# The last chunk as a whole of 512 queries, and W2's load behind the transposes of chunk 1

## The chip, the cores and the metric

The kernel runs on one core of a Trainium2 chip. The core has five engines with an instruction stream each: PE (TensorE, matrix products), DVE (VectorE), ACT (ScalarE), POOL (GpSimd) and SP (SyncE, which here only issues DMAs). PE's weight loads (PEld) run beside its matmuls. Each engine works through its own stream in order; between engines, an instruction waits for semaphores. The metric is the device time of one execution in microseconds, as a median over runs.

## What is computed

Four layers over x of 2048 rows and 512 columns, in bf16 inputs: attention, feed-forward, and the same two again with the same weights. Each adds to x the result of its layer on a normalised x.

```
x = x + A(layernorm(x));  x = x + B(layernorm(x))      # and both once more
A: q, k, v = x @ wqkv (512 x 1536), 32 heads of 16
   scores = q k^T / 4, query i sees keys i-255 .. i    # a sliding window of 256
   softmax over the keys, times v, then @ wo (512 x 512)
B: relu(x @ w1) @ w2                                    # 512 -> 1792 -> 512
```

## The kernel before

**Steps.** The 2048 rows are four chunks of 512 (NCH = 4, L80). Two layers of four chunks make eight steps, k = 0 to 7 (NSTEP, L83). A step is: normalise and transpose the chunk (plan_qkv, L462: xn, then a DMA transpose into xnT), project it to K, Q and V, attend (plan_attention, L532), and then plan_rest (L589): transpose O, multiply by wo, add to x, normalise and transpose again (xn2T), W1 with a ReLU into hT, W2, and add to x, or in the second layer write to the output as ob.

**Attention.** Heads are taken eight at a time (t = 0 to 3). A Unit (L37) is one t for all eight 64-query blocks of a chunk (nq = 8, table FULL, L21) or for half a chunk (nq = 4, table HALF, L28). The tables cut the visible key blocks of a unit into groups: five in FULL, three in HALF. A group is a set of small score matmuls into Sps (all four banks of it), one exponential on ACT from Sps into Pb, and masks on DVE or POOL that zero what the window excludes. Since Sps exists once, the scores of a group wait for the exponential of the group before. When the groups of a unit are masked, P·V matmuls go into a PSUM bank acc, and DVE divides by the sum of the row into O. The two Pb buffers alternate from unit to unit, so a unit's exponentials wait for the P·V matmuls of the unit two before.

The tuple HALVED (L421) names the steps that are attended as two halves of 256 queries: units for all t of the first half, then all t of the second. The same tuple cuts the feed-forward of these steps (L634): W1 is done for columns n0 to n1 of xn2T, 256 or 512 wide, 14 f-blocks of four matmuls each; then W2 for the blocks of 128 rows in that half, 14 matmuls each. In the last step the transposes of O and of xn are done on PE and not by DMA (final, L601).

**Order of work.** Nothing is put in order by hand. Every piece of work is an op (L222) with the engines that could do it, a duration for each as the author estimates it, what it depends on, and a key. A list scheduler in the kernel (from L692) plays the program through with these durations when the program is built, and each engine takes the ready op with the smallest key (on PE) or the smallest time plus key (elsewhere). What it decides is the order in which instructions are written to each engine, and on the chip this order is kept. Scores come before everything on PE (key -1e5), then P·V, then the output projection; projections and feed-forward have keys counted in score groups (first_slot, base), so that they fill PE between groups. The feed-forward of a step has keys from base[k + 1] + 9 to base[k + 1] + 28, that is, during the attention of the next step; the halved one has d0 from its own step's units (L636). K, Q and V of a step have keys 16 groups ahead of the units that need them. Where the scheduler finds PE idle, it writes a dummy matmul (warm, L792).

Limits that the scheduler knows are pools of buffers: four PSUM banks for everything but scores, three xn buffers (L227), three stg, three OT. hT and xn2T exist once, so W1 of a step waits for W2 of the step before. A load is modelled as landed at a fixed time (L231 to L240); such a time only shapes the order, while the chip waits for the DMA itself.

**Loads.** All of x, wqkv, wo, W1 and W2 are loaded at the start by DMAs issued on SP (L131 to L142), in this order: x of chunk 0 in two parts, the three parts of wqkv, x of chunks 1 to 3, wo, W1, W2. The DMA transposes of xn, O and the second xn are issued on SP too. Every matmul and every other instruction goes through one wrapper at L106, so all rows of the profile have that line, and are told apart by their tiles: W1 and W2 are both "w" there, as the program's names are shown without their numbers, W1's matmuls being `ps_d<-xn2T,w` and W2's `ps_d<-w,hT`.

Of the kernel before, what the change touches and what calls it, by code (L numbers as in the profile page):

```python
# [15 lines left out]
P = 128  # L16
# [46 lines left out]
def kernel(  # L63
# [19 lines left out]
    NSTEP = 2 * NCH  # L83
# [31 lines left out]
    pe, dve, act, pool, sp = (InOrder(x) for x in (nc.tensor, nc.vector, nc.scalar, nc.gpsimd, nc.sync))  # L115
# [23 lines left out]
    w1 = const.tile([P, KC, DFF], BF16, name="w1")  # L139
    sp.dma_start(w1[:], B_w1.rearrange("(kc p) n -> p kc n", p=P))  # L140
    w2 = const.tile([P, NF, D], BF16, name="w2")
    sp.dma_start(w2[:], B_w2.rearrange("(f p) n -> p f n", p=P))  # L142


    ident = const.tile([P, P], BF16, name="ident")
# [76 lines left out]
    def op(key, opts, deps=(), take=None, uses=(), keep=0):  # L222
        uses = list(uses) + ([take] if take is not None and take not in uses else [])
        return Op(key, opts, deps, take, uses, keep)
# [6 lines left out]
    def landed(t):  # L231
        o = Op(0, {}, [], None, [], 0)
        fixed.append((o, t))
        return o
# [2 lines left out]
    d_x = [landed(3.95), landed(4.5)]  # L237
    d_w = {1: landed(7.4), 0: landed(9.0), 2: landed(10.6)}
    d_xc = {c: landed(11.4 + 1.7 * c) for c in range(1, NCH)}
    d_wo, d_w1, d_w2 = landed(18.0), landed(24.0), landed(30.0)  # L240


    def copy(e, o, i, relu=False):
# [174 lines left out]
        dve.tensor_tensor(out=x_sb[:, b, :], in0=ps, in1=x_raw(b, b + 1)[:, 0, :] if raw else x_sb[:, b, :], op=ALU.add)  # L418


    HALVED = (0, NSTEP - 1)  # L421
    units, base = [], []
    for k in range(NSTEP):
        base.append(sum(len(u.groups) for u in units))
        for q0, nq in ((0, 4), (4, 4)) if k in HALVED else ((0, 8),):
            units += [Unit(k, k % NCH, t, q0, nq) for t in range(4)]
# [27 lines left out]
    applied, turned = {}, {}  # L454
# [134 lines left out]
    def plan_rest(k):  # L589
# [43 lines left out]
        w1_mm[k], w2_mm[k] = [], []  # L633
        for j0, j1 in ((0, 2), (2, 4)) if k in HALVED else ((0, 4),):  # L634
            if k in HALVED:
                d0 = first_slot[units_of[k][3 + 2 * j0]] + 8  # L636
# [36 lines left out]
    for k in range(NSTEP):  # L673
        plan_attention(k)
        if k == 0:
            plan_qkv(1)
        plan_rest(k)
        if 0 < k < NSTEP - 1:
            plan_qkv(k + 1)
# [274 lines left out]
```

## Time and profile before

| What | us |
|---|---|
| median of 8 runs | 488.06 (485.29 to 488.9) |
| the profiled execution: time | 487.32 |
| the profiled execution: span, first to last instruction | 485.6 |
| PE busy, share of the span | 464.2, 96% |
| DVE / ACT / POOL busy | 367.9 / 337.6 / 316.5 |
| mean granted PE clock | 0.994 |

A row of a timeline or a group reads: start, duration, engine, line, operation, what it writes <- what it reads, shapes, how many; in brackets how long the engine had stood idle before it, and what ended the wait. "<-DMA xnT<-xn" is a DMA transpose that landed. Matmuls overlap, so the spacing between them is shorter than the duration of one. A row of a table of stretches gives, for each engine, its busy time in that stretch with the number of instructions, then the granted PE clock and the share of the DMA engines. SPq rows are DMA issues, and their time is that of issuing, not of the transfer.

### The profile page before, as it was taken

The numbers are of one execution on the slowest core, as the hardware profiler recorded it, in microseconds if no ns is written. First come the engines' busy times: TensorE is split into PE (matmuls) and PEld (weight loads), VectorE is DVE, ScalarE is ACT, GpSimd is POOL, SyncE is SP. The second block draws the span as 40 slices with busy tenths as digits, with TensorE's granted clock in tenths as the row PEclk, the third lists the DMA queues.
The fourth block names the chain that finished last, engine by engine and source line by source line (L and its number), as shares of the span: only waits on it lengthen the run. The fifth ranks groups of instructions, "written<-read, shape, count | busy, mean of one in ns | idle before, by whom it ended". The sixth has DMA issues, their size and how long they took to land.

```text
span 485.6 us, 14677 instructions
## 1 busy us (share of the span) xinstructions
PE 464.2 (96%) x6055; PEld 249.6 (51%) x6055; DVE 367.9 (76%) x965; ACT 337.6 (70%) x281; POOL 316.5 (65%) x716
## 2 busy tenths in 40 slices
PE   7879899998999999999999999999999999999995
PEld 3544555654445545554554554555555455554662
DVE  6969989858898789878989977898758878463111
ACT  3858877878678767876778877777875676755340
POOL 7768878768886788767878767677656557631000
PEclk9989999999999999999999999999999999999999
DMA  8951141004310052002221114020143002100100
GB/s 267 371 58 23 25 66 24 3 1 55 59 22 3 13 78 45 3 1 45 56 36 25 21 31 50 12 46 1 24 88 57 13 1 45 36 12 13 34 23 28
DMA packets 54652, 22.00 MB, mean 45 GB/s; under 512 B 46129, under 2 KB 54065, under 8 KB 54577
## 3 DMA queue, kind: packets, MB, share of 16 engines
q1 hardware_dynamic: 54576, 20.98, 20.4%
q8 instruction: 49, 0.80, 0.7%
q14 instruction: 27, 0.21, 0.2%
HBM read 7.86 MB, written 2.10 MB: 21 GB/s over the span
## 4 chain that ended last, share of the span: by engine, by line
PE 73%; DVE 10%; DMA 7%; POOL 5%; ACT 2%; issue 2%; ACTq 0%; POOLq 0%; DVEq 0%
PE ps_d L106 52%; PE acc L106 12%; PE Sps L106 8%; DMA OT<-O 4%; POOL Pb L106 2%; DMA xnT<-xn 2%; ACT Pb L106 2%; DVE st L106 2%; DVE KBD L106 1%; POOL xn L106 1%; DVE V2f L106 1%; DVE xn L106 1%; DVE Pb L106 1%; DMA xn2T<-xn 1%; DVE Vst L106 1%
## 5 line engine op out<-in xcount | busy, mean ns | idle before, releaser
L106 ACT ACTIVATE Pb<-Sps 128x2048 bf16<-128x2048 f32 (+4 forms) x164 | 283.9, 1731 | 96.2 <-PE Sps L106 72.8
L106 POOL TENSOR_SCALAR_AFFINE_SELECT Pb<-Pb 64x256 bf16<-64x256 bf16 x526 | 226.4, 430 | 96.2 <-ACT Pb L106 73.5
L106 PE MATMUL ps_d<-xn2T,w 128*128 128x512 bf16 (+1 forms) x560 | 110.5, 337 | 1.3 <-DVE hT L106 0.9
L106 PE MATMUL ps_d<-w,hT 128*128 128x512 bf16 x448 | 110.0, 380 | 0.0
L106 PEld LDWEIGHTS <-Pb 128*128 128x128 bf16 x2880 | 83.4, 96 | 24.3 <-issue 7.8
L106 PE MATMUL acc<-V2f,Pb 128*128 128x34 bf16 x2880 | 89.9, 178 | 2.0 <-POOL Pb L106 0.8
L106 PEld LDWEIGHTS <-w 128*128 128x128 bf16 x560 | 50.8, 97 | 39.7 <-issue 4.4
L106 PE MATMUL ps_d<-xnT,wqkv 128*128 128x512 bf16 (+1 forms) x288 | 67.6, 360 | 3.5 <-DVE O L106 2.4
L106 PE MATMUL Sps<-Qt,KBD 32*128 32x192 bf16 (+4 forms) x1536 | 62.5, 249 | 2.5 <-ACT Pb L106 2.2
L106 PEld LDWEIGHTS <-hT 128*128 128x128 bf16 x448 | 40.0, 98 | 44.2 <-issue 2.8
L106 DVE TENSOR_TENSOR Pb<-Pb,tri 128x512 bf16<-128x512 bf16 (+1 forms) x136 | 57.5, 427 | 6.8 <-ACT Pb L106 6.5
L106 DVE TENSOR_SCALAR hT<-ps_d 128x512 bf16<-128x512 f32 (+1 forms) x76 | 47.0, 626 | 11.1 <-PE ps_d L106 10.5
L106 PEld LDWEIGHTS <-KBD 32*128 32x128 bf16 x1536 | 25.7, 92 | 53.4 <-issue 50.3
L106 DVE TENSOR_SCALAR KBD<-ps_d,par 128x256 bf16<-128x256 f32 (+1 forms) x82 | 45.5, 606 | 1.1 <-PE ps_d L106 0.9
L106 ACT ACTIVATE hT<-ps_d 128x256 bf16<-128x256 f32 (+1 forms) x64 | 29.6, 465 | 22.7 <-PE ps_d L106 21.1
L106 DVE BATCH_NORM_STATS2 st<-x_sb 128x6 f32<-128x512 f32 (+1 forms) x64 | 43.7, 683 | 1.2 <-DMA x_sb<-in_A_x_dram 0.8
L106 DVE TENSOR_TENSOR x_sb<-ps_d,x_sb 128x512 f32<-128x512 f32 x48 | 32.8, 685 | 14.3 <-PE ps_d L106 13.8
L106 PEld LDWEIGHTS <-wqkv 128*128 128x128 bf16 x288 | 26.2, 99 | 28.4 <-issue 6.1
L106 DVE TENSOR_TENSOR O<-acc,chk 128x128 bf16<-128x128 f32 x128 | 37.3, 292 | 4.5
L106 DVE RECIPROCAL chk<-acc 128x8 f32<-128x8 f32 x128 | 25.7, 201 | 18.0 <-PE acc L106 15.7
L106 PE MATMUL ps_d<-wo,OT 128*128 128x512 bf16 x128 | 32.9, 380 | 4.0 <-DMA OT<-O 3.8
L106 DVE TENSOR_TENSOR ob<-ps_d,x_sb 128x512 bf16<-128x512 f32 x16 | 11.0, 689 | 31.5 <-PE ps_d L106 31.5
(55 smaller groups left out, 301.1 us busy)
## 6 DMA issues: line engine op xcount, KB each, us to landing
w<-in_B_w_dram SPq DMA_DIRECT2D x2, 1792.0 KB, 13.8
out_dram<-ob SPq DMA_DIRECT2D x16, 128.0 KB, 1.7
wqkv<-in_A_wqkv_dram SPq DMA_DIRECT2D x3, 512.0 KB, 7.0
x_sb<-in_A_x_dram SPq DMA_DIRECT2D x3, 512.0 KB, 8.9
x_sb<-in_A_x_dram SPq DMA_DIRECT2D x2, 256.0 KB, 3.0
wo<-in_A_wo_dram SPq DMA_DIRECT2D x1, 512.0 KB, 8.8
xnT<-xn SPq DMA_TRANSPOSE x28, 2.5
OT<-O SPq DMA_TRANSPOSE x28, 2.5
```

Of the source, the lines that this page charges most:

```text
L106: inst = fn(*a, **k)
```

## The change

Three edits. W2's load is no longer issued with the other loads at the start, but is an op of its own on SP, whose dependence is the four transposes of chunk 1 (`applied[2]` is their list: normalisation 2 is that of step 1's attention); the scheduler places it in SP's order when these have ended in its play-through, with 1.4 us of issue and 9.0 us to landing. The op for the modelled landing of W2 at 30.0 goes. The last step leaves HALVED, so that step 7 has four units of 512 queries with five groups each in place of eight units with three, and its feed-forward is one pass of 512 columns with the keys of the middle steps.

```
@@ -139,7 +139,6 @@
     w2 = const.tile([P, NF, D], BF16, name="w2")
-    sp.dma_start(w2[:], B_w2.rearrange("(f p) n -> p f n", p=P))
@@ -237,7 +236,7 @@
-    d_wo, d_w1, d_w2 = landed(18.0), landed(24.0), landed(30.0)
+    d_wo, d_w1 = landed(18.0), landed(24.0)
@@ -418,7 +417,7 @@
-    HALVED = (0, NSTEP - 1)
+    HALVED = (0,)
@@ -674,6 +673,7 @@
         if k == 0:
             plan_qkv(1)
+            d_w2 = op(0, {"SP": (1.4, lambda: sp.dma_start(w2[:], B_w2.rearrange("(f p) n -> p f n", p=P)), 9.0)}, applied[2])
         plan_rest(k)
```

More of the change, by code (lines that the diff above doesn't have):

```diff
@@ L141 @@
     w2 = const.tile([P, NF, D], BF16, name="w2")
-    sp.dma_start(w2[:], B_w2.rearrange("(f p) n -> p f n", p=P))
     ident = const.tile([P, P], BF16, name="ident")
@@ L239 @@
     d_xc = {c: landed(11.4 + 1.7 * c) for c in range(1, NCH)}
-    d_wo, d_w1, d_w2 = landed(18.0), landed(24.0), landed(30.0)
+    d_wo, d_w1 = landed(18.0), landed(24.0)
     def copy(e, o, i, relu=False):
@@ L418, in residual @@
         dve.tensor_tensor(out=x_sb[:, b, :], in0=ps, in1=x_raw(b, b + 1)[:, 0, :] if raw else x_sb[:, b, :], op=ALU.add)
-    HALVED = (0, NSTEP - 1)
+    HALVED = (0,)
     units, base = [], []
@@ L676 @@
             plan_qkv(1)
+            d_w2 = op(0, {"SP": (1.4, lambda: sp.dma_start(w2[:], B_w2.rearrange("(f p) n -> p f n", p=P)), 9.0)}, applied[2])
         plan_rest(k)
```

## The prediction

> **What bounds the kernel now.** I read the page's busy shares first, then its slices, to see which engine is full and where it is not.
>
> ```profile
> PE 464.2 (96%) x6055; PEld 249.6 (51%) x6055; DVE 367.9 (76%) x965; ACT 337.6 (70%) x281; POOL 316.5 (65%) x716
> ...
> PE   7879899998999999999999999999999999999995
> ...
> PEclk9989999999999999999999999999999999999999
> DMA  8951141004310052002221114020143002100100
> ```
>
> PE is busy 96% of the span. Each slice is 12.1 us; below nine tenths are only some of the first ten and the last, and the third has the lowered clock. So there are two places to look: the start, where PE waits, and everything from about 121 us on, where the sum of PE's work sets the end. The table of stretches says both in us:
>
> ```profile
> core 0: us, PE busy (x) PEld busy (x) DVE busy (x) ACT busy (x) POOL busy (x), PEclk, DMA share, GB/s
> ...
> 25.00:30.00 5.00, 2.16 (x27) 1.34 (x27) 2.13 (x8) 2.76 (x3) 4.39 (x12) 0.92 0.81 92
> 30.00:35.00 5.00, 4.72 (x67) 2.80 (x69) 4.32 (x14) 1.97 (x2) 1.50 (x5) 0.74 0.07 13
> ...
> 378.00:432.30 54.30, 54.30 (x762) 28.61 (x761) 38.30 (x98) 39.35 (x33) 33.50 (x74) 1.00 0.09 21
> ```
>
> The first two stretches are the hole at the start: 2.84 us of idle PE in 25 to 30, then a clock of 0.74. The last is the attention of the last chunk: PE has no idle time at all, so there a shorter wait on another engine is worth nothing and only less PE work counts. (I also read 60 to 378 in eight stretches: PE was busy 310.4 of 318 us, so 7.6 us are lost there, more than half of that before 140 us.)
>
> **Part 1: W2's load leaves the start.** The timeline around the hole:
>
> ```profile
> 21.48 8.20 SPq L106 DMA_TRANSPOSE xnT<-xn  x4
> ...
> 26.95 4.65 POOL L106 TENSOR_SCALAR_AFFINE_SELECT Pb<-Pb 64x256 bf16<-64x256 bf16 x10
> 28.00 0.44 DVE L106 TENSOR_SCALAR xn<-x_sb,mvs,rstds 128x512 bf16<-128x512 bf16 x1 [2.80 <-DMA xnT<-xn]
> ...
> 28.93 2.65 PE L106 MATMUL ps_d<-xnT,wqkv 128*128 128x256 bf16 x12 [2.36 <-DVE O L106]
> ...
> 32.96 1.88 ACT L106 ACTIVATE Pb<-Sps 128x2048 bf16<-128x2048 f32 x1 [2.87 <-PE acc L106]
> ...
> 34.91 1.80 POOL L106 TENSOR_SCALAR_AFFINE_SELECT Pb<-Pb 64x256 bf16<-64x256 bf16 x4 [3.30 <-ACT Pb L106]
> ...
> 35.79 2.50 SPq L106 DMA_TRANSPOSE OT<-O  x2
> ```
>
> Read it as a chain. The first transpose of chunk 1 is issued at 21.48. The fourth xn of chunk 1 needs one of only three xn buffers, so it waits for that transpose to land, 6.50 us later at 27.98 (the longest landing among the xnT rows, whose shortest is 2.4). VectorE stands in front of it for 2.80 us; behind it in VectorE's order is the division that frees a PSUM bank, and PE stands 2.36 us for that. Why the transpose is late shows in the DMA view of 18 to 32 us (40 slices of 0.35 us):
>
> ```profile
> DMA  9999999999999999999999824966920006910000
> GB/s 420 389 391 373 382 354 408 319 354 351 360 360 366 331 357 354 360 318 283 199 146 100 57 28 97 269 18 138 229 47 0 0 0 126 214 35 0 0 0 0
> ```
>
> The engines move loads at some 350 GB/s to about 25 us, a tail runs to 26.4, and only then come the short bursts of the transposes. W1 and W2 are issued at 9.31 and about 11.1 us and land 12.0 and 15.6 us later, so at 21.3 and 26.7: W2 alone takes 5.4 us (1.835 MB, 340 GB/s), and the transpose lands 1.3 us after it. [...] With W2 gone, W1 is done at about 21.3, and the transpose at 21.48 has a free ring: 21.48 + 2.5 (the page's median) = 24.0. VectorE gets to the fourth xn at 25.20 (end of its V2f copies), so its wait becomes **0**, and xn runs at 25.2 in place of 28.0.
>
> What that is worth. PE would start the 12 matmuls when its score matmuls end, at 26.5 in place of 28.93: 2.4 us. They took 2.65 us where eight of the same took 1.05 at 22.78 (about 0.112 each, 1.35 for 12), so the lowered clock cost another 1.3. [...] POOL's ten mask selects run without a gap to 31.60 and are not moved (they follow V2f copies that nothing delayed). The 8 P·V matmuls that now begin at 34.03 need, as I count the masks of the units, the last of them, so can't come before 31.65: 2.4 us. The exponential at 32.96 waits for 24 P·V matmuls that need the masks made up to about 29.7, so about 30.5: 2.4 again. POOL's own next wait of 3.30 us ends with that exponential and absorbs the shift. I take **2.5 us** (floor 0 if another wait closes the hole, ceiling 3.7). Everything later is relative to what went before, since all other loads are in by then, so the shift lasts to the end.
>
> **The moved load's own cost.** In the written order its only DMA comes on SP after the four transposes of chunk 1; the fourth will be issued at 25.7 and take 1.2, so W2 is issued at 26.9, is 1.8 us in issue, and 5.4 us in flight: landed at 34 to 35. First use, on PE, is at 66.3: 30 us of cover. Queued behind it on SP are the transposes of O (35.79 now, 33.3 then): their landing of 2.5 us gives 35.8; behind the tail of W2 plus 1.3 us it is 36.3. The output projection that consumes them starts at 39.51 with no wait, about 37.0 then. So **0**, with 0.7 us to spare; up to 1 us if W2 drags its tail.
>
> **Part 2: the last chunk as a whole.** What is on PE's path:
>
> ```profile
> 412.34 0.40 PE L106 MATMUL Sps<-Qt,KBD 32*128 32x64 bf16 x16
> ...
> 412.67 0.32 PE L106 MATMUL acc<-V2f,Pb 128*128 128x34 bf16 x6
> ...
> 415.09 0.29 PE L106 MATMUL Sps<-Qt,KBD 32*128 32x256 bf16 x4
> ...
> 415.31 1.47 PE L106 MATMUL ps_d<-w,hT 128*128 128x512 bf16 x6
> ...
> 455.98 6.28 PE L106 MATMUL ps_d<-xn2T,w 128*128 128x256 bf16 x56
> ...
> 462.09 6.21 PE L106 MATMUL ps_d<-w,hT 128*128 128x512 bf16 x28
> ```
>
> Durations overlap on PE, so I count from start to next start.
> - Scores: a half unit has three groups of 12, 16 and 4 matmuls, which take 0.34, 0.33 and 0.22, 0.89 in all, and eight units give 7.1 us. A whole unit has five groups, at 0.33 each in a middle chunk (205.28 to 205.61), 1.65, and four units give 6.6: 0.5 less. Each group is also preceded by some 0.1 us in which PE turns from wide matmuls to scores (412.84 plus ten at 0.216 is 415.0, the scores start at 415.09); 20 groups in place of 24 save another 0.4. **0.9 us.**
> - W1: 112 matmuls of 256 columns at 6.28/56 = 0.112 are 12.6 us; 56 of 512 at 0.216 (the same spacing as W2's: 6.21 for 28, less the last one's drain) are 12.1. **0.5 us.**
> - P·V (384), projections, W2 (56), output projection: same counts, 0. Exponentials: 24 become 20, 0.6 us less ACT; evictions of h: 28 at 0.38 become 14 at 0.60, against one W1 group per 0.86 us. Neither is on the path while PE is full.
> - Attention gets shorter for ACT (a pair of half units takes 13.5 us, five groups at 2.55 are 12.7), which only leaves more feed-forward behind it.
> - What it may cost: a middle chunk's PE loses some idle time that the halved one did not (7.6 us over six chunks, most of it early, little after 180); I take 0.1 us and keep 1.2 as its upper end.
>
> **Where the cover could go.** Today the first 256 queries' output projection and norm run beneath the second half's attention. After the change all four blocks start when attention ends: one transpose copy 0.6, projection 0.86, then on VectorE add 0.69 + statistics 0.68 + 0.18 + 0.15 for each block, 6.8 for four, power 0.7, xn 0.55, transpose and copy 1.0, and about 1 for handoffs: some 11.5 us, of which PE itself works 5. So 6.5 us must be filled. At attention's end now (432.4) chunk 6 has done 18 of its 56 W1 matmuls: 38 x 0.216 + 56 x 0.216 = 20.3 us remain. Cover is three times the need, cost 0; without it 6.5 us plus a lowered clock.
>
> **Sum.** 2.5 + 0.9 + 0.5 - 0.1 = 3.8 us. The profiled execution has a span of 485.6 and a time of 487.32 (1.7 around it), which is 0.7 under the runs' median of 488.06. Span 485.6 - 3.8 = 481.8, time 483.5, and against the median **484.3**. 0.3% is 1.5 us, about what a measurement can tell from no change: faster means under 486.6, slower over 489.5.
>
> **Rivals.**
> - A, likeliest, 62%: as summed, 482.8 to 486.
> - B, 7%: the early hole gives back its full 3.7 and attention packs better: 482.
> - C, 12%: the hole stays, another wait in the place of the DMA's (POOL's masks, which end at 31.6, or a transpose still slow behind W1). For: POOL is busy 4.39 of 5 us there. Against: POOL's 3.30 us wait behind it. Only part 2 stays: 488.06 - 1.3 = 486.8; in half of it somewhat better.
> - D, 11%, the other sign: W2 now stands in front of the transposes of O. If it takes the 12.0 to 15.6 us to land that the row shows and not 5.4, it lands at 38.9 to 42.5, the transposes 1.3 later, and PE stands 3.2 to 6.8 us in front of the output projection at 37.0, with a clock drop of 1.3. Net 484.3 + 5 + 1.3 = 490.5. For: the median landing is 13.8. Against: it was queued behind the other loads then. It decides from a landing after about 35.7.
> - E, 8%: the tail's cover is gone, because the order written out for chunk 7 spends chunk 6's feed-forward earlier: decides when less than 6.5 us remain. 484.3 + 6.5 = 490.8.
>
> Chances: faster A, B and half of C, 0.62 + 0.07 + 0.06 = 0.75; same the other half of C and a hundredth of mild D and E, 0.07; slower the rest of D and E, 0.18. The range of eight in ten leaves out B's best and the worse halves of D and E: 481.8 to 489.8; A's own is 482.8 to 486.
>
> **What would show it.** Right: no wait of xn on the xnT transposes near 28, xnT landings near 2.5, no lowered clock in the third slice, W2 landing 7 to 9 us after issue, the second unit pair's exponential near 30.5, W1 rows of 512 columns alone at the end, and no PE idle from the last P·V to the end. Wrong: a wait of PE on OT at 36 to 43, PE idle after the last O, or dummy matmuls there.

## The result

| | before | changed |
|---|---|---|
| median of the runs, us | 487.50 (33 runs) | 484.30 (12 runs) |
| ratio to before | | 0.9938, 95% interval 0.9924 to 0.9952 |
| profiled execution: time / span | 487.32 / 485.6 | 483.38 / 481.7 |
| PE busy | 464.2 | 463.2 |

The change is faster by 0.5 to 0.8%, 3.0 us. In the profiled executions the spans are 3.9 us apart. The kernel before had a median of 488.06 over the eight runs shown first; over all 33 it is 487.50.

The page of the changed kernel, its shares and two rows of its slices (12.0 us each):

```profile
PE 463.2 (96%) x5935; PEld 242.8 (50%) x5935; DVE 366.2 (76%) x960; ACT 337.5 (70%) x268; POOL 313.7 (65%) x708
...
PE   8889899998899999999999999999999999999995
...
PEclk9999999999999999999999999999999999999999
```

The lowered clock of the third slice is gone from the profiled execution: over 25 to 60 us PE's granted clock is 1.00, where the kernel before had 0.95. Over the runs, the mean granted clock is 0.998 in the 14 listed executions of the changed kernel, and 0.994 in 35 of the kernel before. PE is as full as before in the rest, with 120 matmul records fewer (64 score matmuls and 56 of W1). The timeline of the start:

```profile
21.40 5.45 SPq L106 DMA_TRANSPOSE xnT<-xn  x4
...
25.16 0.48 DVE L106 TENSOR_SCALAR xn<-x_sb,mvs,rstds 128x512 bf16<-128x512 bf16 x1
...
26.43 1.52 PE L106 MATMUL ps_d<-xnT,wqkv 128*128 128x256 bf16 x12
...
26.90 0.57 SPq L106 DMA_DIRECT2D w<-in_B_w_dram  x1
...
29.62 1.88 ACT L106 ACTIVATE Pb<-Sps 128x2048 bf16<-128x2048 f32 x1 [1.09 <-PE acc L106]
...
31.68 0.37 PE L106 MATMUL acc<-V2f,Pb 128*128 128x34 bf16 x8 [0.42 <-POOL Pb L106]
...
32.74 2.50 SPq L106 DMA_TRANSPOSE OT<-O  x2
...
36.82 1.03 PE L106 MATMUL ps_d<-wo,OT 128*128 128x512 bf16 x4
```

The fourth xn has no wait, and comes at 25.16 in place of 28.00. The 12 matmuls follow at 26.43 in place of 28.93 and take 1.52 in place of 2.65. The eight P·V matmuls (`acc`) now do wait for POOL's masks, at 31.68; the output projection begins at 36.82 in place of 39.51, without a wait. The DMA view of 18 to 40 us (40 slices of 0.55 us) shows W2 in its new place:

```profile
DMA  9863100048091470942698999999792650010000
GB/s 411 319 208 130 52 0 0 0 81 173 7 202 30 92 146 0 182 86 71 211 305 285 384 363 371 372 356 356 243 220 40 123 115 0 0 30 0 0 0 0
```

The first loads end near 21, and the first three transposes of xn have the engines to themselves: they land 2.5 to 3.3 us after their issue. The fourth, issued at 25.7 and 1.2 us ahead of W2, takes 4.0 and lands at 29.7. W2 runs from about 28 to 34.5 (it lands 7.9 us after its issue, at 34.8), and the two transposes of O land at 35.3 and 36.5. At the other end, the last W1, W2 and out:

```profile
452.17 12.25 PE L106 MATMUL ps_d<-xn2T,w 128*128 128x512 bf16 x56
...
464.26 12.25 PE L106 MATMUL ps_d<-w,hT 128*128 128x512 bf16 x56
...
476.55 0.69 DVE L106 TENSOR_TENSOR ob<-ps_d,x_sb 128x512 bf16<-128x512 f32 x1 [2.33 <-PE ps_d L106]
```

PE has no idle time between the last P·V (423.4) and the end.

**Where the 3.9 us of the two spans lie.** VectorE's instructions are the same, in the same order, up to the last step, so the n-th of one trace can be set beside the n-th of the other. Start times in us, less those of the kernel before; the first row has the time of that row in the kernel before:

```
VectorE instruction   at (before)   changed   W2 moved only   last step whole only
n = 60                   24.3        -0.1         -0.1              0.0
n = 100                  42.9        -2.7         -2.6             +0.8
n = 160                  66.5        -2.7         -2.6             +0.8
n = 180                  75.9        -3.4         -2.6             +0.6
n = 660                 292.0        -3.5         -2.7             +0.3
n = 810                 367.1        -3.2         -2.5             +0.3
end of the span         485.6        -3.9         -2.7             +0.1
```

The first column's -2.7 is the hole at the start, and it stays to the end as forecast. Another 0.7 comes between 66 and 76 us from neither part: there PE stood 1.06 us before the output projection at 68.82 in the kernel before, and not at all in this execution of the changed one, for the same order of instructions (the kernel with W2 alone moved did not gain it). The two rows, before and changed:

```profile
68.82 1.04 PE L106 MATMUL ps_d<-wo,OT 128*128 128x512 bf16 x4 [1.06 <-DMA OT<-O]
```

```profile
65.06 1.04 PE L106 MATMUL ps_d<-wo,OT 128*128 128x512 bf16 x4
```

The transpose of O in front of it landed 4.2 us after its issue in the first and 3.1 in the second. In six other traces with the same order there, PE stood 0.8 to 1.05 us. So this 0.7 is one execution's luck with a transpose's landing. The rest, 0.7 us, comes after 367 us, in the last step; there the kernel with W2 alone moved gained 0.2 as well.

### The profile page after: what moved, and what is told of

Same layout as the page of the kernel before. It is cut to its first block, busy times and chain, and to the rows that moved or that the text cites. A ratio compares the mean times of both kernels' runs of the same rounds, so it can differ in the third digit from the quotient of the medians.

```text
span 481.7 us, 14414 instructions
## 1 busy us (share of the span) xinstructions
PE 463.2 (96%) x5935; PEld 242.8 (50%) x5935; DVE 366.2 (76%) x960; ACT 337.5 (70%) x268; POOL 313.7 (65%) x708
## 4 chain that ended last, share of the span: by engine, by line
PE 71%; DVE 11%; POOL 7%; DMA 6%; issue 2%; ACT 1%; DVEq 0%; POOLq 0%; ACTq 0%
PE ps_d L106 51%; PE acc L106 12%; PE Sps L106 7%; POOL Pb L106 4%; DMA OT<-O 3%; DVE st L106 2%; DVE x_sb L106 2%; DVE KBD L106 2%; DVE Pb L106 1%; ACT Pb L106 1%; POOL xn L106 1%; DVE xn L106 1%; DMA xnT<-xn 1%; DVE V2f L106 1%; DMA xn2T<-xn 1%
## 5 line engine op out<-in xcount | busy, mean ns | idle before, releaser
L106 POOL TENSOR_SCALAR_AFFINE_SELECT Pb<-Pb 64x256 bf16<-64x256 bf16 x518 | 223.1, 431 | 97.6 <-ACT Pb L106 75.7
L106 PE MATMUL ps_d<-xnT,wqkv 128*128 128x512 bf16 (+1 forms) x288 | 66.5, 356 | 2.1 <-DMA xnT<-xn 1.0
L106 PEld LDWEIGHTS <-w 128*128 128x128 bf16 x504 | 45.3, 97 | 44.7 <-issue 5.5
L106 DVE TENSOR_TENSOR Pb<-Pb,tri 128x512 bf16<-128x512 bf16 (+1 forms) x136 | 58.9, 438 | 5.2 <-ACT Pb L106 4.8
L106 DVE TENSOR_SCALAR hT<-ps_d 128x512 bf16<-128x512 f32 (+1 forms) x74 | 45.8, 626 | 11.4 <-PE ps_d L106 10.9
L106 PEld LDWEIGHTS <-KBD 32*128 32x128 bf16 x1472 | 24.1, 92 | 51.6 <-issue 48.9
L106 ACT ACTIVATE hT<-ps_d 128x512 bf16<-128x512 f32 (+1 forms) x52 | 28.5, 552 | 20.9 <-PE ps_d L106 19.3
L106 PEld LDWEIGHTS <-wqkv 128*128 128x128 bf16 x288 | 25.7, 97 | 26.0 <-issue 4.1
```

The lines of the kernel that those rows point to most:

```text
L106: inst = fn(*a, **k)
```

## The experiments

**W2 moved only.** The changed kernel with the last step in two halves. On all engines the instructions stand as in the kernel before, except that W2's issue on SP is behind the four transposes.

```
-    HALVED = (0,)
+    HALVED = (0, NSTEP - 1)
```

> W2's load behind the transposes of chunk 1, the last step still in two halves; every other instruction stands where it stood before. The prediction's first part says 2.5 us less (about 485.0, ratio 0.995), with the fourth xn at 25.2 and the output projection of the first block near 36.9 in place of 39.5. If another wait closed the hole instead, the time would be that of before.

Measured: 484.68 us, ratio 0.9950 (0.9933 to 0.9967), span 482.9. Its timeline:

```profile
25.18 0.48 DVE L106 TENSOR_SCALAR xn<-x_sb,mvs,rstds 128x512 bf16<-128x512 bf16 x1
...
26.45 1.52 PE L106 MATMUL ps_d<-xnT,wqkv 128*128 128x256 bf16 x12
...
30.16 1.46 PE L106 MATMUL ps_d<-xnT,wqkv 128*128 128x512 bf16 x6 [0.58 <-DMA xnT<-xn]
...
31.71 0.37 PE L106 MATMUL acc<-V2f,Pb 128*128 128x34 bf16 x8
...
36.85 1.03 PE L106 MATMUL ps_d<-wo,OT 128*128 128x512 bf16 x4
```

The hole's size is what was forecast, 2.5 us (2.64 in the trace, 2.4 in the ratio), out of the change's 3.0. One small wait stands beside the moved load: the fourth transpose of xn landed 4.3 us after its issue here, and PE stood 0.58 us for it. It costs next to nothing, since the P·V matmuls behind it come at 31.71, and POOL's masks would let them start no earlier than about 31.7 (31.68 in the changed kernel, where PE stood for the masks). Whether W2's load, issued 1.2 us behind that transpose, is what slows it was not tested.

**Last step whole only.** The kernel before with the last step whole. The order is that of the changed kernel but for W2's place.

```
-    HALVED = (0, NSTEP - 1)
+    HALVED = (0,)
```

> The last step whole, W2 still loaded at the start; every other instruction stands as in the changed kernel. The prediction's second part says 1.3 us less (about 486.2, ratio 0.9973). From the two traces, whose spans differ by 3.9 us and which are 2.7 us apart by the first output projection, it may be as little as 0.7 or as much as 1.2. If the whole form had no worth of its own, the time would be that of before.

Measured: 487.13 us, ratio 1.0004 (0.9986 to 1.0023), span 485.7. No gain of 1.3 us is there: the interval ends at 0.7. The span of this one execution can't be read against the other's, since its start, which is the same program as before, came out 0.8 us later. The wait of xn, and the table of stretches:

```profile
28.54 0.41 DVE L106 TENSOR_SCALAR xn<-x_sb,mvs,rstds 128x512 bf16<-128x512 bf16 x1 [3.38 <-DMA xnT<-xn]
...
29.45 2.72 PE L106 MATMUL ps_d<-xnT,wqkv 128*128 128x256 bf16 x12 [2.92 <-DVE O L106]
```

```profile
25.00:30.00 5.00, 1.63 (x23) 1.04 (x20) 1.59 (x6) 2.47 (x2) 4.39 (x12) 0.77 0.71 91
30.00:35.00 5.00, 5.00 (x53) 2.83 (x51) 3.82 (x15) 1.81 (x2) 1.39 (x4) 0.55 0.14 26
```

VectorE's wait was 3.38 us in place of 2.80, which is 0.5 of the 0.8; and the clock lost 0.23 x 5 + 0.45 x 5 = 3.4 us, twice the 1.7 of the kernel before (0.08 x 5 + 0.26 x 5, from the 0.92 and 0.74 of its table of stretches). The median is not explained by such a start: the mean granted clock over the runs is the same in both kernels, 0.994. From n = 690 of VectorE (307 us) on, where the start plays no part, this kernel takes 0.3 us less than before, and the changed one 0.6 less than the one with W2 alone moved.

Counting PE's matmuls there from start to next start, without idle time, in the two traces shows what the last step's form did (from n = 690 to PE's last matmul; before, and changed):

```
rows of PE                   before    changed   difference
Sps (scores)                  14.38     13.89      -0.49
ps_d<-xn2T,w (W1)             50.04     49.47      -0.57
ps_d<-w,hT (W2)               52.98     52.78      -0.20
acc (P.V)                     22.89     23.02      +0.13
transposes of O                0.89      1.01      +0.12
projections                   30.30     30.49      +0.19
transposes of xn, count        0.93      0.92      -0.01
sum of work                  172.4      171.6      -0.8
idle (transposed O)            0.68      0.76      +0.1
```

A row's figure includes the turn from it to what comes next, so W1's 0.57 is not yet W1's own. The sums repeat: 172.4 with W2 alone moved, and 171.6 with the last step whole alone. So the whole form's worth is shown by the rows of the traces (0.8 us of work, of which idle time takes back some) and by no time measured here.

**The two halvings apart.** The last feed-forward in halves and attention whole; then attention in halves and the feed-forward whole.

```
+    FEED_HALVED = (0, NSTEP - 1)
-        for j0, j1 in ((0, 2), (2, 4)) if k in HALVED else ((0, 4),):
+        for j0, j1 in ((0, 2), (2, 4)) if k in FEED_HALVED else ((0, 4),):
                 d0, d1 = base[k + 1] + 9, base[k + 1] + 28
+                if k in FEED_HALVED:
+                    d0, d1 = d0 + 9.5 * (j0 // 2), d0 + 9.5 * (j0 // 2) + 9.5
```

> The changed kernel, with only the last W1 and W2 in two halves again (W1 of 256 columns, first half before the second); attention stays whole and every instruction before the last feed-forward stands as in the changed kernel. By the spacing of W1's rows (0.112 against 0.216 for twice the columns) it is 0.45 to 0.6 us slower than the changed kernel, 484.8. If the whole form's worth is all in the attention, it is as the changed kernel.

```
+    UNITS_HALVED = (0, NSTEP - 1)
-        for q0, nq in ((0, 4), (4, 4)) if k in HALVED else ((0, 8),):
+        for q0, nq in ((0, 4), (4, 4)) if k in UNITS_HALVED else ((0, 8),):
```

> W2 moved, attention of the last step in halves, its feed-forward whole. Counted from start to start over the last 173 us, the kernel with W2 alone moved and the changed one differ by 0.5 us in scores, 0.2 in what precedes a score group, 0.6 in W1, and the whole attention gives back 0.3 in other switches and 0.2 to 0.5 in the wait for the transposed O. So whole attention is worth 0 to 0.2 us, W1 0.6, and this kernel is level with the changed one within 0.3 us, 484.3 to 484.6; by the prediction's own terms (0.9 less 0.1 for the attention) it would be 485.1.

Measured: 485.04 us, ratio 0.9934 (0.9917 to 0.9951), and 484.76 us, ratio 0.9929 (0.9911 to 0.9947). By time neither can be told from the changed kernel. The count of PE's rows can: with only the feed-forward halved, W1's row is 49.60 in place of 49.47 and all other work as in the changed kernel; with only the attention halved, W1's row is 49.90 and all other rows of work as before. So W1's own width is worth **0.14 us**, and whole attention 0.65. The turns can be counted too. From a wide matmul's start to the first score matmul's start are 0.311 us, where the next wide matmul would start after 0.216, so such a turn costs 0.095. With attention whole, 32 score groups follow a wide matmul in place of 36: 0.38 us less. (W1's and W2's rows fall by 0.43 and 0.20, which is more, because two of their turns go over to the projections, whose rows rise by 0.19.) Whole attention is then 0.49 in scores and 0.38 in turns, less 0.25 which P·V and the transposes of O give back. The first kernel was expected 0.45 to 0.6 us slower through W1's width, which the rows do not show. The expectation for the second had W1 at 0.6 and the attention near 0: by these rows it had them the wrong way round, and its time of 484.76 is 0.2 above the 484.3 to 484.6 expected, which these runs can't tell apart.

**A buffer of its own for the fourth xn.** The kernel before, W2 at the start. The fourth xn of chunk 1 is written to an unused part of the hT tile, so that it waits for no transpose. The order is that of before.

```
+        own = (lid, j) == (2, 3)
-            box.t = box.tile([P, D], BF16, "xn")
+            box.t = spare()[:, KC, :] if own else box.tile([P, D], BF16, "xn")
```

> The kernel before with W2 at the start, but the fourth xn of chunk 1 in a buffer of its own (an unused part of the hT tile), so that it waits for no transpose; the order of instructions is that of before. The theory of the buffer: VectorE's 2.8 us at 25.2 are gone though the transposes still land near 28, and 2.0 to 2.7 us are gained, as with the moved load. The rival, that it is the late xnT itself which holds PE: the stall moves to chunk 1's projections and less than 1 us is gained.

Measured: 485.46 us, ratio 0.9975 (0.9955 to 0.9995), span 483.3. Its timeline:

```profile
25.20 0.50 DVE L106 TENSOR_SCALAR xnT<-x_sb,mvs,rstds 128x512 bf16<-128x512 bf16 x1
...
25.73 1.19 SPq L106 DMA_TRANSPOSE xnT<-xnT  x1
...
26.49 1.53 PE L106 MATMUL ps_d<-xnT,wqkv 128*128 128x256 bf16 x12
...
30.81 1.46 PE L106 MATMUL ps_d<-xnT,wqkv 128*128 128x512 bf16 x6 [1.19 <-DVE O L106]
...
32.10 0.36 PE L106 MATMUL acc<-V2f,Pb 128*128 128x34 bf16 x8
```

and its landing of the fourth transpose:

```profile
xnT<-xnT SPq DMA_TRANSPOSE x1, 4.9
```

xn (written to the tile that is also xnT) is at 25.20 and the 12 matmuls at 26.49, as in the changed kernel, though the transposes still land 4.5 to 6.4 us after their issue. Then chunk 1's first full-width projections come at 30.81, where they came at 29.80 with W2 moved: PE idles 1.19 us there. The row puts that down to a division, but the division ended at 29.8. The fourth transpose, which these matmuls read, was issued at 25.73 and landed 4.95 us later, at 30.68; 0.13 us after it the matmuls start. In the changed kernel they start 0.14 us after its landing (29.66), with W2 alone moved likewise (30.02 and 30.16). So here it is the transpose that is waited for. The eight P·V matmuls behind it come at 32.10, 0.4 us after the masks would let them (31.7). In the table by VectorE's instructions this kernel is at about -2.3 from n = 100 on. So the wait for the xn buffer was what made the hole, and the late landing itself is worth 0.4 us more.

**W1's load moved too.** The changed kernel with W1 issued behind the transposes, in front of W2, which makes rival D happen.

```
-    sp.dma_start(w1[:], B_w1.rearrange("(kc p) n -> p kc n", p=P))
-    d_wo, d_w1 = landed(18.0), landed(24.0)
+    d_wo = landed(18.0)
+            d_w1 = op(0, {"SP": (1.4, lambda: sp.dma_start(w1[:], ...), 9.0)}, applied[2])
```

> The changed kernel with W1's load moved behind the transposes too, in front of W2's; else the same order. This is rival D made to happen. If transposes of O wait in the ring for the loads in front of them: W1 and W2 are 10.8 us in flight from about 27.5, done near 39, the transposes of O issued at 32.7 land near 40 in place of 35.2, PE waits 3 to 4 us in front of the output projection at 36.8, and the time is 487 to 490. If transposes are served beside the loads: 484.3 as the changed kernel.

Measured: 488.47 us, ratio 1.0032 (1.0008 to 1.0057), span 486.9. Its timeline, and the row of its landings of O's transposes up to 60 us (shortest, median, longest):

```profile
32.60 4.10 SPq L106 DMA_TRANSPOSE OT<-O  x2
...
40.12 1.24 PE L106 MATMUL ps_d<-wo,OT 128*128 128x512 bf16 x4 [3.21 <-DMA OT<-O]
```

```profile
DMA to landing us min/median/max: 6.8/7.1/7.5
```

W2 was done at 39.6 us (12.1 us after its issue at 27.5), the transposes landed in 7 us in place of 2.5, PE stood 3.21 us, and from 40.8 the clock stood at half for 3.413 us. The time is 4.2 us above the changed kernel's. In each of the three traces the first transpose queued behind a load lands only when that load has: at 27.98 after 26.77 in the kernel before, at 35.32 after 34.84 in the changed one, at 40.07 after 39.59 here. So the transposes waited behind the loads issued before them, at both places, and W2's place is good only because its 1.8 MB end in time, at 34.84: the projection that reads O's first transpose is at 36.82.

**The output projection later.** The changed kernel; the scheduler is told that a transpose of O takes longer, so that more work stands between it and the projection in PE's order. The chip's transpose is the same. 3.6 first, then 3.1 and 4.6, then 3.6 in the kernel before.

```
                 t = op(-5, {"SP": (1.22, lambda j=j, to=to: sp.dma_start_transpose(
-                    out=to(), in_=O_of[k][:, j, :]..., 2.6)}, ready, ob, [ob])
+                    out=to(), in_=O_of[k][:, j, :]..., 3.6)}, ready, ob, [ob])
```

> The changed kernel with the scheduler told that a transpose of O takes 3.6 us in place of 2.6, so that the output projection stands later in PE's order. The waits of PE for the transposed O in the changed kernel are 2.6 us in four places after 60 us. If they are time lost, up to 2.6 us are gained (481.7); if PE is the bound whatever the order, less than 1; the order of all later work changes with it, by which it may also lose 1 to 2.

> The changed kernel with 3.1 in place of 2.6 for a transpose of O in the scheduler's play-through. If the gain at 3.6 (ratio 0.9854) came from the output projection standing later, about half of its 4 us is seen, 482 to 483. If it was the luck of another order, anything from 480 to 487.

> The same with 4.6. If later is better as far as the transpose is covered, it is level with the kernel at 3.6, 480.5 to 481.5; by the luck of the order, anything from 480 to 487.

> The kernel before with 3.6: W2 at the start, the last step halved. If the worth of the later projection is independent of the change, 3 to 4 us less than before, 484; and the distance of 3 us between this kernel and the changed one at 3.6 is the change's own worth once more.

| scheduler's figure for the transpose of O | us | ratio to before |
|---|---|---|
| changed kernel, 2.6 | 484.30 | 0.9938 (0.9924 to 0.9952) |
| changed kernel, 3.1 | 480.71 | 0.9875 (0.9843 to 0.9907) |
| changed kernel, 3.6 | 481.02 | 0.9854 (0.9829 to 0.9878) |
| changed kernel, 4.6 | 481.83 | 0.9891 (0.9859 to 0.9923) |
| kernel before, 3.6 | 486.13 | 0.9977 (0.9958 to 0.9997) |

Three of three values make the changed kernel faster, by 2.5 to 3.6 us, and the kernels at 3.1 and 3.6 are the fastest of this study. The reason given for it doesn't hold as stated. In the waits of PE after 60 us at 3.6, the changed kernel's 2.6 us before the transposed O have become 2.2, and another wait is larger:

```profile
PE Sps L106 <- ACT Pb L106: 3.2, 7, 0.9
PE ps_d L106 <- DMA OT<-O: 2.2, 2, 1.8
```

PE's idle time over the whole execution is 11.8 us in both traces; what fell is work, by 2.1 us, of which 1.4 are in the rows of the dummy matmuls (four less, 34 in place of 38) and 0.7 in W2's rows (four turns to scores fewer are 0.4 of it); the other rows cancel. The traces at 3.1 and 4.6 miss some matmul records, so their work can't be summed. But they hold at least 36 and 40 dummy matmuls: at 4.6 no fewer than 38, and that kernel is faster too, so fewer dummies aren't the common cause either. At 3.1 half the gain was expected and all of it came. In the kernel before, 3 to 4 us were expected and the same figure gives 1.1, a third of what it gives in the changed one. That the changed kernel is faster with these larger figures is shown; whether the later projection itself does it, or the other order of all later work that comes with it, stays open.

## Why the prediction was right, point by point

**The hole at the start** (2.5 us forecast, floor 0, ceiling 3.7): right in its mechanism and its size. The move alone gives 2.64 us in the trace and 2.4 in the ratio. The chain was buffer, VectorE, division, PE; the spare buffer takes away its first link alone and gets 2.3 of it. That the 3.7 us of wait and clock (2.4 and 1.3) would not all be had, because POOL's masks end at 31.6, is seen in the wait that appeared there (0.42 at 31.68, against the forecast 31.65). One link was read wrongly without harm: the second unit pair's exponential was to come near 30.5, because its P·V matmuls would need masks made up to 29.7. They started at 28.78, right after the mask that ended at 28.73, and the exponential came at 29.62. The wait that binds is the next one. Rival C falls, and B's larger gain too.

**The clock.** The lowered clock was to vanish with the wait, and in the profiled execution it did. In the kernel before, it came 0.3 us after a wait of PE of 2.36 us had ended, and stood at half for 3.413 us. The 1.3 us that the forecast put to it, from 2.65 us for the 12 matmuls, are 1.1 in the traces, where the same 12 take 1.52 in the changed kernel. More on the clock below.

**The moved load** (cost 0): right. It landed at 34.8, O's first transpose at 35.3, and the projection that reads it came at 36.82 without a wait. The sign "xnT landings near 2.5" was met by two of four, the first taking 3.3 us and the fourth 4.0, which the masks hid. Rival D was wrong about where W2 would end, right about the mechanism: with twice the bytes it came about, with 3.2 us of wait, the lower end of D's 3.2 to 6.8, and 488.5 us in place of D's 490.5.

**The last step as a whole** (1.3 us forecast): the mechanism was right, that less PE work is what counts there, and the size was not; 0.3 and 0.6 us are counted in the two pairs of traces (the kernel before and the one with the last step whole; the one with W2 alone moved and the changed one). Term by term:
- Scores, 0.5: measured 0.49.
- Turns in front of score groups, 0.4: measured 0.38. But P·V and the transposes of O, which the forecast put at 0, take 0.13 and 0.12 us more from start to start. In the whole form they come in other groups, and the forecast counted no turn but the one.
- W1's width, 0.5: measured **0.14**. This is the step that failed. The text says that it counts from start to next start, and then divides a merged row's 6.28 us by its 56 matmuls. That duration runs 0.17 us past the start of the next row; from its start at 455.98 to the next row's at 462.09 are 6.11, so 0.109 each and 12.2 us for 112, against 12.1 for the 56 wide ones (452.17 to 464.26 after). The same correction had been made for W2's row in the same line.
- Idle time, 0.1: 0.5 and 0.2 in the two pairs (0.68 to 1.22, and 0.56 to 0.76), all of it before the transposed O.

**The tail's cover** (rival E): did not come about. At the last division (425.9) chunk 6's W1 still had 44 matmuls to do and all of its W2, 21.6 us, above the forecast 20.3, and PE never stood. The last transposed block was ready at 442.83, 9.3 us before it was needed at 452.17.

**The sum.** 484.3 was forecast and 484.30 measured, and that is closer than the terms are. Part 2 was some 0.9 us too large (1.3 against 0.3 to 0.6), and the median that the sum was taken from was 0.6 us above that of all runs; the two errors have opposite signs. The 3.9 us between the profiled spans, too, match the forecast 3.8 only with 0.7 us of luck at 66 to 76 us in them.

## What to carry to other kernels

A load that nobody needs yet was not free here: W2, issued at about 11.1 us and first read at 66.3, landed at 26.77, and the short transpose issued behind it at 21.48 landed only at 27.98; through a pool of three buffers that stopped VectorE for 2.80 us and then PE for 2.36. Place such a load behind the small transfers that are urgent, and check that it ends before the next urgent ones have to be there; in the same place loads of twice the size cost 4.2 us, more than the 2.4 to 2.6 that the move had gained. When costing a change of instruction width on a full PE, take the distance from one row's start to the next row's start, never a merged row's duration over its count, count every kind of turn and not only the one that the change is after (here 0.095 us for each turn from wide matmuls to scores), and take into the sum what the rows that do the same matmuls in other groups give back.

## What the runs showed of the hardware that was not expected

At some waits of PE the granted clock went to half (0.50 in the record of the kernel before), for 3.413 us in some of these executions and for 6.827 in others, and not for the same time behind the same instructions. From the clock records of the profiled executions, before the last 20 us: the kernel before had 3.413 us at half rate from 29.2 us on; the one with the last step whole, which begins with the same instructions, had 6.827 us from 27.7; the kernel before with the later projection 6.827 from 26.9; the kernel with W1 moved too had 3.413 from 40.8, at its wait for the transposed O. Each stands at a wait of PE, of 2.36, 2.92, 2.36 and 3.21 us in this order. In the first and the last, half rate begins 0.3 and 0.7 us after the wait has ended; in the other two it begins within the wait, 1.2 and 0.4 us after its start. In the changed kernel, with W2 alone moved, with the spare buffer, in both halved forms, and at 3.1 and 3.6 there was none; the longest idle time among these is 1.78 us, at 118.9 in the kernel at 3.6. The kernel at 4.6 doesn't fit in: it had 3.413 us from 124.4, after an idle time of 1.59 us in its trace. That trace misses matmul records, so how long PE really stood there isn't known, and no threshold can be taken from these runs.

Two executions with the same wait of PE, 2.36 us, thus had 3.413 us at half rate and 6.827 (the kernel before, and that kernel with the later projection, whose VectorE has the same order to 42 us). The second 3.413 us are 1.7 us of lost clock, but 2.0 of the 6.8 us lie in the wait itself, where PE has nothing to do, and only about 0.2 us reached the end of that stretch: at 40.8 us VectorE was 0.16 us later, where it had been 0.05 us earlier at 30.2. With the last step whole it was 0.3, the other 0.5 of its late start being the longer wait.
